# Last output layer of two chained MLPs: six of its seven token tiles as seven block products instead of eight, the sums of h and of weights made by GpSimd

## The chip, the cores and the metric

The kernel runs on one core of a Trainium2 chip. Its time is the device time of one execution in microseconds (us); lower is better. TensorE (PE in the profile) does the matmuls into PSUM banks, VectorE (DVE) and ScalarE (ACT) the elementwise work, GpSimd (POOL) is a third elementwise engine that takes its operands from SBUF, and SyncE (SP) issues the DMAs. Each engine works through its own queue in order and waits on semaphores of the others.

## The reference

Attention with mixed heads gives x of 1792 tokens by 768; two MLPs follow, and the output of the second is the result:

```
h = x @ w_in;    g = elu(h);        x = g @ w_out       # first MLP,  768 -> 2048 -> 768
h = x @ w_in2;   g = relu(h)**2;  out = g @ w_out2      # second MLP, 768 -> 2048 -> 768
```

All arrays are float32 at the kernel's door. This case is about the last product, `g @ w_out2`, for the second half of the tokens (896 of them).

## The kernel before, in words

Attention comes first, then both MLPs for the first 896 tokens, then both for the second 896. Each float32 operand of a matmul is split into a high part (`hi`, a cast to fp32r) and a low part (`lo` = the value minus `hi`, also fp32r), and a product is three matmuls: hi by hi, lo by hi, hi by lo (`three`, L661 to L666). The cast is ACT's (L518 for weights, L669 for h), the subtraction is DVE's (L525 for weights, L670 for h), and both inputs of that subtraction lie in SBUF.

The last stage is `outer_last(1)` (L935). h is kept raw in 16 tiles `hr`, one for each block of 128 of the 2048 rows of the inner dimension, 896 tokens wide. For each half `nh` of the 768 output columns and each of the 16 blocks `f`, one weight tile (128 by 384) and one h tile are split, and for each of the seven token tiles of 128 three matmuls with 384 columns are issued, the h part being the stationary operand: 2 x 16 x 7 x 3 = 672 matmuls. At the end of each half seven banks are copied out, by DVE and ACT in turn, and stored. Weights come from DRAM (`w2of`) through six buffers `wf`; a buffer can be loaded again when its `hi` and `lo` have been made. The parts lie in five buffers `wh`/`wl` and four `rh`/`rl`, which TensorE frees. `Weights.load_ahead` sets how far ahead loads are issued, `Weights.part` makes the two parts of the next weight tile, `split_ahead` those of the next h tile.

The stage ahead of it, `seven(1, ...)` (L732), makes h with seven block products (Strassen's scheme in Winograd's form); its last pieces end on DVE in lines L753 to L801 (sums of a PSUM bank and a saved tile) and L693 (squares, both inputs in SBUF).

Of the kernel before, what the change touches and what calls it, by code (L numbers as in the profile page):

```python
# [8 lines left out]
F32 = mybir.dt.float32  # L9
# [15 lines left out]
FU = DM // 2  # L25
# [356 lines left out]
class Weights:  # L382
# [5 lines left out]
    def __init__(self, nc, dram, w1i, w1o, w2i, w2o):  # L388
# [14 lines left out]
        for k in (k1i, k2i):  # L403
            self.units += [(name, k, q, STATIONARY) for q in range(FC // 2) for name in self.SEVEN]
            if k is k1i:
                self.units += [("f32", k1o[:, f, t * FU : (t + 1) * FU], None, STATIONARY) for t in range(2) for f in range(FC)]
        self.units += kept
        self.raw, self.single, self.parts, self.keep, self.quad, self.aside, self.extra = {}, {}, {}, [], {}, [], []
# [8 lines left out]
    def load(self, room=None):  # L417
        i = self.loaded
        self.loaded += 1
        kind, src, kept, _ = self.units[i]  # L420
        if kind == "f64":
            self.raw[i] = self.load_raw(src, room)
        elif kind == "f32":
            self.single[i] = self.plain()
            self.nc.sync.dma_start(out=self.single[i], in_=src)
        elif kind == "a11":
            of = self.quad[kept, id(src)] = {}
            for j, name in ((2, "a21"), (3, "a22"), (0, "a11"), (1, "a12")):
                of[name] = self.plain("aq", 4) if j < 2 else self.plain()
                self.nc.sync.dma_start(out=of[name], in_=src[4 * kept + j])  # L430
# [78 lines left out]
    def part_hi(self):  # L509
        i = self.done  # L510
        kind, start = self.units[i][0], self.units[i][3]
        if kind in self.SEVEN:
            self.single[i] = self.combine(*self.units[i][1:3], kind)
        f = self.single[i]
        n = f.shape[1]
# [18 lines left out]
    def load_ahead(self, i):  # L534
        self.flush()
        while self.loaded < len(self.units):
            if self.loaded > i + (self.LOAD if self.units[self.loaded][0] not in self.SEVEN else len(self.SEVEN)):
                break
            self.load()
# [23 lines left out]
def col(i):  # L563
    return slice(i * 128, (i + 1) * 128)


class Mlps:
# [164 lines left out]
    def seven(self, m, x, carry=()):  # L732
# [23 lines left out]
        for q in range(FC // 2):  # L756
            a, b, c, d, e = (self.bank()[:, :S] for _ in range(5))
            plan = (("b11", a), ("t1", b), ("b21", a), ("b22", b), ("t2", c), ("t3", d), ("t4", e))
            for i, (name, p) in enumerate(plan):
# [50 lines left out]
                del carry[:3]  # L810
                if q == FC // 2 - 1 and i in (2, 4):
                    self.split_ahead(i // 4)
        for step in range(7 * FC // 2, 7 * FC // 2 + 3):
# [121 lines left out]
    def outer_last(self, half):  # L935
# [28 lines left out]
        return x if half == 0 else None  # L964

    def run(self):
        with ExitStack() as ctx:
# [22 lines left out]
        self.hr = {}  # L990
        self.start_split(STATIONARY)
        self.seven(1, x, carry)
        self.outer_last(1)

# [48 lines left out]
```

## Time and profile before

| | us |
|---|---|
| median of 3 runs (lowest to highest) | 1278.42 (1274.05 to 1279.73) |
| the profiled execution, its own time | 1277.57 |
| its span, first to last instruction | 1275.7 |
| PE busy in the span | 1233.7 |
| DVE, ACT, POOL busy | 943.1, 679.3, 52.4 |
| mean granted clock of TensorE | 0.996 of full speed |

The time of the profiled execution lies 1.87 us above its span, which is what is around the instructions. Matmul durations in the records overlap each other (each is pipelined into the next), so for TensorE the distance from one start to the next is read, not the duration.

### The profile page before, as it was taken

Reading aid. Unit: us, or ns where it says so; the run is one execution under the profiler, and the core shown is the slowest. Engines: PE = TensorE matmul, PEld = TensorE weight load, DVE = VectorE, ACT = ScalarE, POOL = GpSimd, SP = SyncE. Lnnn points to the kernel's source line nnn. Section 1 sums busy time; section 2 is a strip of 40 time slices with the busy share of each in tenths; the row PEclk is TensorE's granted clock in tenths of the full one; section 3 lists DMA queues with packets and bytes.
Section 4 is the critical chain, followed back from the end, with each engine's and each line's share of the span. In section 5 each row is a group of like instructions: output and inputs, shape, how many; then the busy total and the mean of one; then the engine's idle time right before and its main releaser. Section 6 shows DMA issues by size and latency. Waiting matters only on the chain.

```text
span 1275.7 us, 35064 instructions
## 1 busy us (share of the span) xinstructions
PE 1233.7 (97%) x14295; PEld 1101.7 (86%) x14296; DVE 943.1 (74%) x1974; ACT 679.3 (53%) x1476; POOL 52.4 (4%) x118
## 2 busy tenths in 40 slices
PE   9999989999789999999999999999999999999998
PEld 4677777777579999988899999999999998999998
DVE  4577667777759998778999996868874559887452
ACT  4666666666537774333444554546663445454342
POOL 1011010110410000000000000000000000000000
PEclk9999999999999999999999999999999999999999
DMA  6666646555635545666666555131221111212131
GB/s 186 201 204 195 208 161 205 185 171 184 203 108 177 174 155 162 191 184 199 224 222 227 186 174 171 49 119 50 69 75 55 51 50 50 75 44 85 34 105 44
DMA packets 124121, 179.02 MB, mean 140 GB/s; under 512 B 25177, under 2 KB 103353, under 8 KB 123961
## 3 DMA queue, kind: packets, MB, share of 16 engines
q1 hardware_dynamic: 123720, 176.50, 43.0%
q8 instruction: 112, 1.84, 0.6%
q14 instruction: 49, 0.39, 0.1%
q10 hardware_dynamic: 240, 0.29, 0.1%
HBM read 101.86 MB, written 36.18 MB: 108 GB/s over the span
## 4 chain that ended last, share of the span: by engine, by line
PE 76%; DVE 11%; ACT 6%; DMA 3%; issue 3%; SPq 0%; ACTq 0%; DVEq 0%; POOL 0%; POOLq 0%
PE ps_qk L664 5%; PE ps_qk L666 5%; PE ps_qk L665 5%; PE ps_pv L665 5%; PE ps_pv L666 5%; PE ps_pv L664 5%; PE ps_post L664 5%; PE ps_post L666 5%; PE ps_post L665 5%; PE ps_mix L664 5%; PE ps_mix L666 5%; PE ps_mix L665 5%; PE ps_mix L182 4%; PE ps_post L218 4%; PE ps_pv L254 3%; PE ps_qk L156 3%
## 5 line engine op out<-in xcount | busy, mean ns | idle before, releaser
L518 ACT CAST wh<-wf 128x384 fp32r<-128x384 f32 (+1 forms) x272 | 133.3, 492 | 209.6 <-DVE wf L477 129.4
L525 DVE TENSOR_TENSOR wl<-wf,wh 128x384 fp32r<-128x384 f32 (+1 forms) x272 | 144.7, 534 | 76.4 <-ACT wh L518 74.7
L218 PEld LDWEIGHTS ps_post<-wg,ex 60*64 60x64 f32 x5040 | 139.5, 135 | 51.2 <-issue 30.2
L192 ACT ACTIVATE ex<-ps_mix,nmax 128x448 f32<-128x448 f32 x180 | 112.6, 630 | 117.5 <-DVE nmax L190 117.4
L670 DVE TENSOR_TENSOR rl<-hr,rh 128x896 fp32r<-128x896 f32 x96 | 104.5, 1089 | 54.4 <-ACT rh L669 54.4
L218 PE MATMUL ps_post<-wg,ex 60*64 60x60 f32 x5040 | 135.0, 220 | 6.5 <-issue 4.9
L236 DVE COPY at<-ps_post 128x420 f32<-128x420 f32 x178 | 97.6, 591 | 53.8 <-PE ps_post L218 51.1
L182 PE MATMUL ps_mix<-graw,pre 64*64 64x448 f32 (+1 forms) x720 | 113.6, 557 | 13.8 <-ACT ex L192 6.3
L190 DVE TENSOR_REDUCE nmax<-ps_mix 128x1 f32<-128x448 f32 x180 | 104.5, 616 | 24.3 <-PE ps_mix L182 23.9
L669 ACT CAST rh<-hr 128x896 fp32r<-128x896 f32 x96 | 90.1, 939 | 50.3 <-PE ps_post L666 25.1
L254 PE MATMUL ps_pv<-at,v 64*64 64x110 f32 (+3 forms) x2976 | 100.0, 249 | 5.3 <-issue 2.9
L254 PEld LDWEIGHTS ps_pv<-at,v 64*64 64x64 f32 x2976 | 88.4, 134 | 14.9 <-issue 6.5
L156 PE MATMUL ps_qk<-kt,qt 64*64 64x448 f32 (+1 forms) x680 | 92.6, 543 | 1.5 <-ACT sc L161 1.2
L447 ACT ACTIVATE wf<-wd 128x384 f32<-128x384 f32 (+1 forms) x134 | 68.1, 512 | 42.8 <-DMA wd<-w1o 24.0
L161 ACT COPY sc<-ps_qk 120x448 f32<-120x448 f32 x167 | 80.7, 539 | 11.1 <-PE ps_qk L156 11.1
L477 DVE SCALAR_TENSOR_TENSOR wf<-wd,wf 128x384 int32<-128x384 int32 (+1 forms) x134 | 67.7, 509 | 3.9
L475 DVE SCALAR_TENSOR_TENSOR wf<-wd,wf 128x384 int32<-128x384 int32 (+1 forms) x134 | 67.7, 509 | 3.8
L182 PEld LDWEIGHTS ps_mix<-graw,pre 64*64 64x64 f32 (+1 forms) x720 | 34.7, 134 | 32.7 <-ACT ex L192 16.6
L684 ACT ACTIVATE tmp<-tmp 128x448 f32<-128x448 f32 x48 | 27.9, 581 | 57.2 <-DVE tmp L794 43.9
L664 PE MATMUL ps_qk<-xh,wh 128*128 128x448 f32 x150 | 55.3, 369 | 0.3 <-DVE tmp L691 0.3
L666 PE MATMUL ps_qk<-xh,wl 128*128 128x448 f32 x150 | 55.0, 367 | 0.0
L665 PE MATMUL ps_qk<-xl,wh 128*128 128x448 f32 x150 | 55.0, 367 | 0.0
(247 smaller groups left out, 3152.1 us busy)
## 6 DMA issues: line engine op xcount, KB each, us to landing
graw<-sc SPq DMA_DIRECT2D x180, 210.0 KB
wd<-w1i SPq DMA_DIRECT2D x32, 384.0 KB
wd<-w1o SPq DMA_DIRECT2D x48, 256.0 KB
wd<-w2i SPq DMA_DIRECT2D x32, 384.0 KB
wf<-w2of SPq DMA_DIRECT2D x48, 192.0 KB
wd<-w2o SPq DMA_DIRECT2D x22, 384.0 KB
w1if<-wf SPq DMA_DIRECT2D x32, 192.0 KB
w1of<-wf SPq DMA_DIRECT2D x48, 128.0 KB
```

The source lines that it names most:

```text
L156: nc.tensor.matmul(out[a][x:y], qt[n][o, p, x:y], k[o, p, :], start=True, stop=True)
L182: nc.tensor.matmul(out[r][64 * g : 64 * g + 64], pre64[o], e[g][o], start=True, stop=True)
L190: nc.vector.tensor_reduce(nmax, p, AX.X, ALU.max, negate=True)
L192: nc.scalar.activation(e, p, AF.Exp, bias=nmax, scale=1.0, accum_out=tot[s][:, r : r + 1])
L218: nc.tensor.matmul(out[g][y, 6 if c == 3 else 2 * c + r], e[rows][o, key : key + 64], w[o, rows], start=True, stop=True)
L254: nc.tensor.matmul(p, vt[b, i // 3][y, jc, g % 6 * D : (g % 6 + 1) * D], m, start=(jc == 0), stop=(jc == JC - 1), skip_group_check=True)
L518: self.nc.scalar.copy(hi, f)
L525: self.nc.vector.tensor_tensor(lo, self.single.pop(i), hi.bitcast(F32), ALU.subtract)
L664: mm(p, wh, xh, start=first, stop=False)
L665: mm(p, wh, xl, start=False, stop=False)
L666: mm(p, wl, xh, start=False, stop=last)
L670: self.nc.vector.tensor_tensor(lo, raw, hi.bitcast(F32), ALU.subtract)
```

## The change

The 896 tokens are seven tiles of 128. Tiles 0 to 2 and tiles 4 to 6 become the two row blocks of a 2 by 2 block product (A11, A12 and A21, A22 of h, cut along the inner dimension after block 8; B11, B12, B21, B22 of the weights, cut likewise and at column 384); tile 3 is multiplied as before. The seven products are, in this order: n = 0, A11 B11; n = 1, S1 T1; n = 2, A12 B21; n = 3, S4 B22; n = 4, S2 T2; n = 5, S3 T3; n = 6, A22 T4. Each has 8 steps, one for each inner block. The sums S (of h) and T (of weights) are made by GpSimd in float32 from the raw tiles, and ACT and DVE split them as they split raw tiles. For that the raw weights are kept until GpSimd has read them, and B12 and B21 are loaded a second time into a `spare` of four tiles. Tile 3 takes part in n = 0 (with B11 and B12), 2 and 3. The blocks of the output are put together from banks and saved tiles at the end of each product, by ACT, DVE and, in six places, GpSimd.

```
-        self.units += kept
+        first, second = kept[:FC], kept[FC:]
+        self.made, self.keep_raw, self.k2o = {}, {}, k2o
+        half = FC // 2
+        self.units += [u for f in range(half) for u in (first[f], second[f])]
+        self.units += [("made", ("t1", f), None, MOVING) for f in range(half)]
+        self.units += first[half:] + second[half:]
+        self.units += [("made", (name, f), None, MOVING) for name in ("t2", "t3", "t4") for f in range(half)]
+        self.last = len(self.units) - 8 * half
...
+            if i >= self.last:
+                self.keep_raw[i] = self.single[i]
...
+            if self.loaded >= self.last and self.loaded > i + self.LOAD - 1:
+                break
...
-                if q == FC // 2 - 1 and i in (2, 4):
-                    self.split_ahead(i // 4)
+                if q == FC // 2 - 1 and i in (2, 4, 6):
+                    if m == 0:
+                        if i < 6:
+                            self.split_ahead(i // 4)
+                    else:
+                        self.part_last(0, i // 2 - 1)
...
+    def part_last(self, n, f):
+        a = (STATIONARY - H_AT) % LINE // 4
+        t = self.sums[f] if n in (1, 4) else self.hr[f + (FC // 2 if n in (2, 3, 6) else 0)]
+        t = t[:, 512:] if n == 6 else t[:, : 512 if n in (0, 2, 3) else 384]
+        parts = [self.hq.tile([128, 2 * S + LINE // 4], F32R, name=f"r{x}", bufs=4)[:, a : a + t.shape[1]] for x in "hl"]
+        self.split(*parts, t)
+        self.halves[n, f] = parts
+    def seven_last(self):
...
+        for k, (n, f) in enumerate(steps):
...
+            if n == 0:
+                weights = [w.take(), w.take()]
+            else:
+                weights = [w.take()]
+            taken.append((f, hi, lo, weights))
+            tail = n == 6 and half - 3 <= f < half - 1
+            if not tail:
+                for i in range(3):
+                    for g, hi, lo, weights in taken:
+                        self.three(p[i], hi[:, col(i)], lo[:, col(i)], *weights[0], n not in (2, 3) and g == 0,
+                                   n in (2, 3, 4, 5, 6) and g == half - 1, True)
+                    if n == 6 and f == half - 1:
+                        o = room()
+                        tt(o, u[i], p[i], ALU.subtract)
+                        put(o, 4 + i, 0)
+                if n in (0, 2, 3):
+                    for j, y in enumerate(weights):
+                        q = j if n == 0 else n - 2
+                        self.three(rest[q], hi[:, col(3)], lo[:, col(3)], *y, n == 0 and f == 0, n > 0 and f == half - 1, True)
+                taken.clear()
+            if n == 0:
+                sub(ta[f], w.keep_raw[at + 1], w.keep_raw[at], ALU.subtract)
+                sub(self.sums[f], self.hr[f][:, 512:], self.hr[f + half][:, 512:], ALU.add)
+            elif n == 1:
+                sub(self.sums[f], self.sums[f], self.hr[f][:, :FU], ALU.subtract)
+            elif n == 2:
+                sub(self.hr[f + half][:, :FU], self.hr[f + half][:, :FU], self.sums[f], ALU.subtract)
+            elif n == 3:
+                sub(ta[f], w.keep_raw[at], ta[f], ALU.subtract)
+                sub(tb[f], w.keep_raw[at], aux["b12", f], ALU.subtract)
+            elif n == 4:
+                sub(self.hr[f][:, :FU], self.hr[f][:, :FU], self.hr[f][:, 512:], ALU.subtract)
+            if (n, f) >= (5, 1) and (k - 41) < half:
+                sub(ta[k - 41], ta[k - 41], aux["b21", k - 41], ALU.subtract)
+            if 21 <= k < 21 + half:
+                load("b12", k - 21, FC + k - 21)
+            if 38 <= k < 38 + half:
+                load("b21", k - 38, half + k - 38)
+            w.load_ahead(w.used)
+            while w.done < min(len(w.units), w.used + 4):
+                w.part()
+            if k + 3 < len(steps):
+                self.part_last(*steps[k + 3])
+            if f < half - 1:
+                continue
+            for i in range(3):
+                if n == 0:
+                    copy(one_a[i], p[i])
+                elif n == 1:
+                    copy(one_b[i], p[i])
+                elif n == 2:
+                    out(p[i], i, 0, copies[i % 2])
+                elif n == 3:
+                    copy(both[i], p[i])
+                elif n == 4:
+                    tt(u[i], p[i], one_a[i], ALU.add)
+                    o = room()
+                    sub(o, both[i], u[i], ALU.add)
+                    put(o, i, 1)
+                elif n == 5:
+                    tt(u[i], p[i], u[i], ALU.add)
+                    o = room()
+                    sub(o, u[i], one_b[i], ALU.add)
+                    put(o, 4 + i, 1)
+            if n in (2, 3):
+                out(rest[n - 2], 3, n - 2, copies[n - 2])
...
-        self.start_split(STATIONARY)
+        self.halves, self.k2o = {}, w.k2o
         self.seven(1, x, carry)
-        self.outer_last(1)
+        self.seven_last()
```

In the changed kernel the same helpers stand 11 to 13 lines lower (L529 and L536 split weights, L682 and L683 split h, L677 to L679 are the three matmuls). `sub` is GpSimd's tensor_tensor, `tt` is DVE's.

Where instructions stand now. GpSimd's queue, at the start of the last stage, before: after the weighing of attention's last step (`wg`) there is nothing but the end of the program.

```order
L659 TENSOR_TENSOR xl_6961<-tmp_7343,xh_6960 128x448
L202 TENSOR_TENSOR wg_7617<-post_87,rec_7615 128x120
L1039 UNCONDITIONAL_BRANCH
```

The same place in the changed kernel, the first four of 70 new instructions of this kind, and the first four of n = 3 (`xh` and `xl` are the rooms of the sums, `wf` raw weights, `hr` raw h):

```order
L202 TENSOR_TENSOR wg_7617<-post_87,rec_7615 128x120
L1059 TENSOR_TENSOR xh_15966<-wf_15877,wf_15854 128x384
L1060 TENSOR_TENSOR xl_15967<-hr_14955,hr_15491 128x384
L1059 TENSOR_TENSOR xh_15966<-wf_15915,wf_15895 128x384
L1060 TENSOR_TENSOR xl_15967<-hr_15008,hr_15544 128x384
...
L1066 TENSOR_TENSOR xh_15966<-wf_16461,xh_15966 128x384
L1067 TENSOR_TENSOR xl_15967<-wf_16461,xh_15966 128x384
L1066 TENSOR_TENSOR xh_15966<-wf_16484,xh_15966 128x384
L1067 TENSOR_TENSOR xl_15967<-wf_16484,xh_15966 128x384
```

DVE's queue, from the last square of the stage ahead into the first steps of the last stage, before:

```order
L693 TENSOR_TENSOR hr_15956<-tmp_15959 128x448
L525 TENSOR_TENSOR wl_15974<-wf_15879,wh_15973 128x384
L525 TENSOR_TENSOR wl_15978<-wf_15897,wh_15977 128x384
L670 TENSOR_TENSOR rl_15982<-hr_15089,rh_15981 128x896
L525 TENSOR_TENSOR wl_16009<-wf_15917,wh_16008 128x384
L670 TENSOR_TENSOR rl_16013<-hr_15142,rh_16012 128x896
```

And in the changed kernel; a step of n = 0 now takes two weight tiles and one narrower h tile, and four weight parts stand ahead of the first of these h tiles:

```order
L706 TENSOR_TENSOR hr_15954<-tmp_15961 128x448
L536 TENSOR_TENSOR wl_15999<-wf_15895,wh_15998 128x384
L536 TENSOR_TENSOR wl_16003<-wf_15915,wh_16002 128x384
L536 TENSOR_TENSOR wl_16007<-wf_15936,wh_16006 128x384
L536 TENSOR_TENSOR wl_16011<-wf_15992,wh_16010 128x384
L683 TENSOR_TENSOR rl_16015<-hr_15142,rh_16014 128x512
L536 TENSOR_TENSOR wl_16040<-wf_15994,wh_16039 128x384
L536 TENSOR_TENSOR wl_16044<-wf_15996,wh_16043 128x384
L683 TENSOR_TENSOR rl_16048<-hr_15223,rh_16047 128x512
```

SyncE's queue in the changed kernel around the end of n = 2 (`wf` are first loads of weights, `xh` second loads into `spare`, `out` the four stores of that end): a second load of B12 and the first loads of B22's last two tiles now stand behind the four stores.

```order
L434 DMA wf_16579<-w2of_68 128x384
L1017 DMA out<-tmp_16589 128x384
L1017 DMA out<-tmp_16592 128x384
L1017 DMA out<-tmp_16595 128x384
L1017 DMA out<-tmp_16598 128x384
L1013 DMA xh_15966<-w2of_68 128x384
L434 DMA wf_16616<-w2of_68 128x384
```

## Rows read from the trace of the kernel before

**Rows 1.** The page, part 1: busy us, share of the span, instructions.

```profile
PE 1233.7 (97%) x14295; PEld 1101.7 (86%) x14296; DVE 943.1 (74%) x1974; ACT 679.3 (53%) x1476; POOL 52.4 (4%) x118
```

**Rows 2.** Windows of the last stage: us, busy of each engine, clock, DMA.

```profile
1155.20:1213.40 58.20, 58.20 (x337) 58.19 (x337) 30.70 (x42) 24.18 (x38) 0.00 (x0) 1.00 0.21 64
1213.40:1271.90 58.50, 58.47 (x338) 58.15 (x336) 24.50 (x31) 20.03 (x31) 0.00 (x0) 1.00 0.18 59
```

**Rows 3.** Timeline of PE, first and last matmuls of the stage: start, us, engine.

```profile
1155.03 0.36 PE L666 MATMUL ps_qk<-eh,wl 128*128 128x448 f32 x1
1155.23 0.34 PE L664 MATMUL ps_mix<-wh,rh 128*128 128x384 f32 x1
1155.40 0.34 PE L665 MATMUL ps_mix<-wl,rh 128*128 128x384 f32 x1
...
1271.53 0.34 PE L666 MATMUL ps_post<-wh,rl 128*128 128x384 f32 x1
```

**Rows 4.** Groups of the last stage by form: count, busy us, mean ns, idle before.

```profile
L670 DVE TENSOR_TENSOR rl<-hr,rh 128x896 fp32r<-128x896 f32 x30 | 32.7, 1091 | 9.0 <-ACT rh L669 9.0
L669 ACT CAST rh<-hr 128x896 fp32r<-128x896 f32 x30 | 28.1, 937 | 2.1 <-PE ps_post L665 2.1
L525 DVE TENSOR_TENSOR wl<-wf,wh 128x384 fp32r<-128x384 f32 x31 | 17.2, 556 | 38.3 <-ACT wh L518 38.3
L518 ACT CAST wh<-wf 128x384 fp32r<-128x384 f32 x30 | 15.3, 512 | 53.0 <-PE ps_pv L666 27.4 <-PE ps_post L666 24.0 <-issue 1.7
```

**Rows 5.** Timeline, 349 to 352 us and 329 us: DVE beside POOL.

```profile
349.32 1.15 POOL L659 TENSOR_TENSOR xl<-tmp,xh 128x448 fp32r<-128x448 f32 x1 [6.60 <-ACT xh L658]
350.15 0.72 DVE L525 TENSOR_TENSOR wl<-wf,wh 128x384 fp32r<-128x384 f32 x1 [0.84 <-ACT wh L518]
350.42 1.46 POOL L659 TENSOR_TENSOR xl<-tmp,xh 128x448 fp32r<-128x448 f32 x1
350.80 1.49 DVE L525 TENSOR_TENSOR wl<-wf,wh 128x384 fp32r<-128x384 f32 x1
...
329.56 2.22 POOL L659 TENSOR_TENSOR xl<-tmp,xh 128x448 fp32r<-128x448 f32 x2 [2.07 <-DMA tmp<-xd]
329.85 0.87 DVE L197 TENSOR_SCALAR tot<-tot 128x2 f32<-128x2 f32 x1
```

**Rows 6.** Timeline of DVE into the last stage, before.

```profile
1151.36 1.08 DVE L670 TENSOR_TENSOR rl<-hr,rh 128x896 fp32r<-128x896 f32 x1
1152.37 0.61 DVE L793 TENSOR_TENSOR tmp<-ps_post,tmp 128x448 f32<-128x448 f32 x1
...
1155.21 0.55 DVE L525 TENSOR_TENSOR wl<-wf,wh 128x384 fp32r<-128x384 f32 x1
1155.68 0.61 DVE L753 TENSOR_TENSOR tmp<-tmp,ps_qk 128x448 f32<-128x448 f32 x1
1156.21 1.69 DVE L693 TENSOR_TENSOR hr<-tmp 128x448 f32<-128x448 f32 x3
...
1158.29 0.55 DVE L525 TENSOR_TENSOR wl<-wf,wh 128x384 fp32r<-128x384 f32 x1
1158.76 1.08 DVE L670 TENSOR_TENSOR rl<-hr,rh 128x896 fp32r<-128x896 f32 x1
1159.76 0.55 DVE L525 TENSOR_TENSOR wl<-wf,wh 128x384 fp32r<-128x384 f32 x1
```

**Rows 7.** Weight loads: SP's issue, then GB/s from 1140 to 1160 us in half-us slices.

```profile
1148.46 0.32 SPq L425 DMA_DIRECT2D wf<-w2of  x1
...
GB/s 0 0 0 0 0 0 0 0 0 0 0 0 0 0 0 0 0 0 22 169 203 0 25 249 363 151 0 0 0 0 126 264 3 87 243 80 0 0 58 280
```

**Rows 8.** Single lines, ns min/median/max: L659; L525 in the last stage; L197.

```profile
L659 POOL TENSOR_TENSOR xl<-tmp,xh x12: 1122/1136/1455, 329.6 to 356.2; 128x448 fp32r<-128x448 f32 x12
L525 DVE TENSOR_TENSOR wl<-wf,wh x34: 549/557/559, 1149.9 to 1254.2; 128x384 fp32r<-128x384 f32 x34
L197 DVE TENSOR_SCALAR tot<-tot x90: 156/160/874, 23.1 to 354.6; 128x2 f32<-128x2 f32 x90
```

**Rows 9.** POOL's groups by form over the whole span.

```profile
L202 POOL TENSOR_TENSOR wg<-post,rec 128x120 f32<-128x120 f32 x90 | 34.8, 387 | 291.2 <-DVE rec L199 221.2 <-PE ps_mix L182 61.1 <-PE ps_qk L156 8.9
L659 POOL TENSOR_TENSOR xl<-tmp,xh 128x448 fp32r<-128x448 f32 x12 | 13.7, 1162 | 13.6 <-ACT xh L658 11.5 <-DMA tmp<-xd 2.1
```

**Rows 10.** Timeline of the end, before.

```profile
1271.91 0.56 DVE L961 COPY tmp<-ps_post 128x384 f32<-128x384 f32 x1 [0.48 <-PE ps_post L666]
```

More of the change, by code (lines that the diff above doesn't have):

```diff
@@ L513, in part_hi @@
             self.single[i] = self.combine(*self.units[i][1:3], kind)
+        if kind == "made":
+            self.single[i] = self.made[self.units[i][1]]
         f = self.single[i]
@@ L964, in outer_last, with rooms, load, put @@
         return x if half == 0 else None
+    def part_last(self, n, f):
[6 more added lines that the diff above has]
+    def seven_last(self):
+        nc, w = self.nc, self.weights
+        copy, tt, sub = nc.scalar.copy, nc.vector.tensor_tensor, nc.gpsimd.tensor_tensor
+        k2o, half = self.k2o, FC // 2
+        def rooms(pool, tag, n):
+            room = pool.tile([128, n], F32, name=tag, tag=tag)
+            return [room[:, i * FU : (i + 1) * FU] for i in range(n // FU)]
+        high, low = (rooms(self.xp, f"x{x}", KC * 2 * S + LINE // 4) for x in "hl")
+        ta, spare, tb, self.sums = high[:8], high[8:12], low[:8], low[8:14] + high[12:14]
+        kept = [rooms(self.ep, f"e{x}", 9 * S) for x in "hl"]
+        one_a, one_b, both, u = kept[0][:3], kept[0][3:6], kept[0][6:9], kept[1][:3]
+        for name, of in (("t1", ta), ("t2", ta), ("t3", tb), ("t4", ta)):
+            for f in range(half):
+                w.made[name, f] = of[f]
+        aux = {}
+        def load(name, f, i):
+            aux[name, f] = spare[f % 4]
+            nc.sync.dma_start(out=spare[f % 4], in_=k2o[i])
+        def put(o, i, nh):
+            r = 2 * S + i * 128
+            nc.sync.dma_start(out=self.out[r : r + 128, nh * FU : (nh + 1) * FU], in_=o)
+        def room():
+            return self.tmp()[:, :FU]
+        def out(p, i, nh, engine):
+            o = room()
+            engine(o, p)
+            put(o, i, nh)
+        copies = nc.vector.tensor_copy, copy
+        steps = [(n, f) for n in range(7) for f in range(half)]
+        banks = [[self.bank()[:, :FU] for _ in range(3)]]
+        rest = [self.bank()[:, :FU] for _ in range(2)]
+        taken = []
+        for k, (n, f) in enumerate(steps):
+            at = w.used
+            hi, lo = self.halves.pop((n, f))
+            if f == 0 and n in (1, 4, 5, 6):
+                banks.append([self.bank()[:, :FU] for _ in range(3)])
+            p = banks[(0, 1, 0, 1, 2, 3, 4)[n]]
+            if n == 0:
[59 more added lines that the diff above has]
+                    tt(u[i], p[i], u[i], ALU.add)
+                    o = room()
+                    sub(o, u[i], one_b[i], ALU.add)
+                    put(o, 4 + i, 1)
+            if n in (2, 3):
+                out(rest[n - 2], 3, n - 2, copies[n - 2])
```

## The prediction

> **What bounds the kernel now.** First the page's busy times [rows 1]: PE works in 97% of the span, so what counts is what reaches PE. Then the windows of the last stage [rows 2]: PE is busy in all but 0.03 us of 116.7 at a granted clock of 1.00, DVE in 55.2, ACT in 44.2, POOL in none. The stage is bound by matmuls alone. Its timeline [rows 3] gives the price of one: from the first start, 1155.23, to the last of 672, 1271.53, is 116.30 us over 671 distances, 0.1733 us each. The groups [rows 4] say what feeds it: one h part (DVE 1.09 us) and one weight part (0.56 us) for every 3.64 us of matmuls, with waits on DVE and ACT that are theirs, not PE's. From the page alone, fewer matmuls would be time won. But the change hands 70 sums to POOL, and the last view to read is how POOL and DVE run side by side [rows 5].
>
> **What it removes.** Product 0 has 15 matmuls a step (three tiles, and tile 3 with two weight tiles), products 2 and 3 have 12, products 1, 4, 5 and 6 have 9: 8 x (15 + 24 + 36) = 600 instead of 672. At 0.1733 us [rows 3], 72 matmuls are **12.5 us**, and a step lasts 2.60, 2.08 or 1.56 us on PE: 104.0 us in all.
>
> **What it adds on ACT and DVE.** 64 weight tiles are split instead of 32, and 56 h tiles of 512 (24 of them) or 384 columns instead of 32 of 896. DVE takes 0.47 us from the start of a 384-column part to that of the next instruction (1158.29 to 1158.76) and 1.00 for 896 (1158.76 to 1159.76) [rows 6], so 0.60 for 512: some 118 parts are about 60 us, plus 9 for banks, of 104. ACT stays below that [rows 4]. Alone, both hide under PE, but for the start: the third weight tile is wanted after 15 matmuls, at 1157.8, while DVE still has the squares of the stage ahead to do (1156.21 and 1.69 us long [rows 6]). Two h parts ahead of them become 0.4 us shorter, one of 0.6 is added: the part would be there at about 1158.2. That costs 0.4 us.
>
> **What it adds on DMA.** 16 second loads of 192 KB, and the same 14 stores. DMA engines are busy for 0.21 and 0.18 of the stage [rows 2], so the amount is free. A load takes some 2.0 us: issued at 1148.46, its bytes move in the slices up to 1150.5 [rows 7]. The place in the queue is not free, see product 3.
>
> **What it adds on POOL, and what that does to DVE.** The span has no POOL sum of 384 columns. 448 columns take 1136 ns (median [rows 8]), 120 take 387 [rows 9]: 2.28 ns a column, so 384 take 0.99 us. 70 of them are 69 us of 104, which alone would hide. The trace shows that they are not alone. While two POOL sums ran, two weight parts of DVE, 0.56 us at any time in the last stage [rows 8], took 0.72 and 1.49, and the second POOL sum 1.46 [rows 5]. Taking each undisturbed length from its end gives when it really began: DVE 350.32, POOL 350.74, DVE 351.74. So they took turns: DVE's part kept POOL away for 0.42 us, POOL's sum of 448 columns kept DVE away for 1.00. Scaled to 384 columns POOL holds for 0.86 us; a DVE part of 512 holds for 0.56. A tiny DVE operation shows the same: 0.87 us beside a POOL sum [rows 5], 0.16 usually [rows 8]. Every weight part and h part of the last stage reads two SBUF tiles, as the held ones did; so do the squares. DVE's operations that read a bank did not show it.
>
> The Trainium skill, "SBUF — State Buffer", section "Who interferes with whom", states this as a rule against such a change: a DVE instruction with two SBUF inputs and a GpSimd instruction that reads SBUF use one shared read interface under an exclusive lock, kept for the whole instruction. That they take turns, the trace agrees [rows 5]. By "the whole instruction" a pair would cost the recorded 0.56 + 0.99 = 1.55 us and the sum would be the long-hold rival below; by the rows it is 1.28. The measurement decides.
>
> **The sum in turns.** In us a step, DVE's holds and POOL's against PE's: product 0, 1.40 + 1.72 = 3.12 against 2.60; product 1, 0.84 + 0.86 = 1.70 against 1.56; product 2, 0.98 + 0.86 = 1.84 against 2.08; product 3, 0.98 + 1.72 = 2.70 against 2.08; products 4 and 5, 1.70 against 1.56; product 6, 0.84 against 1.56. What decides is how many sums stand ready, because each ready one delays one DVE part: then a step of two parts costs 2.56 to 2.70 us, and the lead of two to three steps that the buffers allow is used up. By product:
>
> Product 0. POOL may start at about 1150.0, when PE has read the last of the tiles whose room the sums take. Six sums find their data there, 5.2 us of holds; four DVE operations on banks (0.6 each) hide about two of them. The third weight part comes at about 1161.1 instead of 1158.2, and PE's second step 3.3 us late. In the other seven steps 0.52 us each is missing, 3.6; 1.4 of it the lead covers. Together **+5.5**.
>
> Products 1 and 2. S2 overwrites S1, and S4 overwrites A12, which must be split before: POOL has one sum a step to do and DVE's lead rather pays 1 us and gets it back. **0**.
>
> Product 3. The 16 sums T2 and T3 and the 8 sums S3 wait for nothing that DVE does; some start in the second half of product 2. Eight steps at 2.70 instead of 2.08 are 5.0 late. In SP's queue the fourth second load of B12 and the last two first loads stand behind the four stores of product 2, whose copies stand behind delayed parts on DVE: POOL and then DVE stop until they land, some 2 us with neither at work. Product 2's lead gives 2.6 back. **+4.4**.
>
> Product 4. About nine sums are left, so five of its steps cost 2.56 instead of 1.56: 5.0, less 0.3 of lead, **+4.7**.
>
> Product 5. Three sums for stores and seven T4 are ready, again five steps at 2.56: 5.0, less 1.5 of lead, **+3.5**.
>
> Product 6. One sum is left; its part is wanted only at the last step. **0**. The end is as before: one DVE operation on a bank after the last matmul (1271.91 to 1272.47 [rows 10]) and a store.
>
> Added, 18.1 us; removed, 12.5. Against the profiled execution's own 1277.57 that is +5.6: **1283 us**, 0.36% above the median of the runs, 1278.42, which itself is 0.85 above that execution.
>
> **The bounds.** Below: if port and engines never stop, the holds decide. All eight-step sums are 108.8, six sums for stores 5.2, squares and one other of the stage ahead 2.4; without product 6 (6.7), in which PE is the slower one, and the h part already made (0.6), 109.1 us from 1150.0 is 1259.1, and product 6 adds 12.5: PE ends at 1271.6, as it does now (1271.7). That is 1277.5 us. Above: 0.27 us more for each of 70 pairs by recorded lengths is 19 us: 1302. The kind of work is that of [rows 5] (the same DVE instruction, POOL one size wider), so I stay near the holds that they show.
>
> **The rivals.**
> No turns: the meeting of [rows 5] was something else and the sums hide. For it: POOL has 35 us to spare, DVE 35. Against it: two independent DVE forms and POOL itself show it. Then 12.5 less 0.4: 1265.5 us, faster. Point of decision: DVE's weight parts stay at 0.56 us while POOL works.
> Tight turns: the 18.1 shrinks since POOL's early sums go into DVE's idle time and the lead never breaks. 1277.5 us, no change. Point of decision: the stops in products 3 and 5 don't appear.
> Long holds: a pair costs its recorded 1.55 us. For it: POOL's own records are rough, and a chain of alternate waits may lose something at each hand-over. Against it: the two turns of [rows 5]. 1302 us, slower. Point of decision: stage sum of DVE's and POOL's busy times equals its length.
>
> **How the numbers follow.** The turns as summed: 0.55, with a range of its own of 1277 to 1291 (half the lead's cover either way, and 0.1 us on each of 70 pairs). Tight turns 0.13, no turns 0.16, long holds 0.11, a wait that I don't see 0.05. A measurement of this kernel can tell about 0.5%, 6.4 us, from no change: below 1272.0 is faster, above 1284.8 slower. Faster is no turns, 0.16. Of the forecast's 0.55 some 0.36 lies below 1284.8; with tight turns that is the same, 0.49. Slower is 0.19 of the forecast, long holds and the unseen wait: 0.35. The range takes in no turns at its low end and reaches to 1293, where about 0.15 is left above it.
>
> **What the profile of the changed kernel would show.** The matmul count of the stage, 600, at 0.173 us where they run on. DVE's weight parts in the stage at a mean near 1 us instead of 0.56, with many at about 1.4 in products 0, 3, 4 and 5, and near 0.56 in product 6. PE's idle time in the stage near 18 us, ended by DVE's parts: a gap of some 3 us after the first step, none to speak of in products 1, 2 and 6. POOL sums at 0.99 us or, waiting, up to 1.4. A DVE mean near 0.56 there would refute the turns; PE gaps ended by POOL itself or by SP's loads would mean another wait than mine; a clock below 1.00 in these gaps would add what I have not counted.

## The result, and the profile after

| | kernel before | changed kernel |
|---|---|---|
| median (lowest to highest) of 15 executions of each | 1277.16 us (1270.61 to 1285.45) | 1282.98 us (1279.22 to 1292.57) |
| ratio of the two, with its 95% interval | | 1.0054 (1.0027 to 1.0080) |
| the profiled execution, its own time | 1277.57 us | 1292.57 us |
| first matmul of the last stage | 1155.23 us | 1164.44 us |
| length of the last stage on PE (first to last start, and one matmul more) | 116.47 us | 122.59 us |

The change makes the kernel 0.5% slower, by 5.8 us between the medians; 1283 us with +5.6 was forecast. The profiled execution of the changed kernel is the slowest of its 15. Of the 15.0 us by which it is longer than that of before, 9.2 lie ahead of the last stage, where they were not followed, and executions of the kernel before differ by as much among themselves. So the stage is compared, not the span: 122.59 - 116.47 = **6.1 us longer**, though it has 72 matmuls fewer.

The page of the changed kernel, its busy times (us, share of the span, instructions), answers to [rows 1]. The windows of the last stage below it answer to [rows 2], with the same columns.

```profile
PE 1240.2 (96%) x14224; PEld 1092.8 (85%) x14224; DVE 1001.6 (78%) x2034; ACT 696.0 (54%) x1537; POOL 141.0 (11%) x188
```

```profile
1164.40:1287.10 122.70, 110.77 (x602) 105.80 (x600) 113.88 (x133) 60.60 (x129) 83.56 (x67) 0.97 0.28 87
```

Before, PE was busy in all of this stage and DVE in half of it. Now PE stands still for 11.9 us of 122.7, its mean clock is 0.97, and DVE is busy in 113.9 us. A page that shows DVE at 93% with the other engines waiting for it seems to say that DVE has too much work. It does not, and the next two views tell why. The groups of DVE and POOL in the last stage (with columns as in [rows 4]):

```profile
L683 DVE TENSOR_TENSOR rl<-hr,rh 128x512 fp32r<-128x512 f32 x22 | 30.5, 1386 | 0.0
L536 DVE TENSOR_TENSOR wl<-wf,wh 128x384 fp32r<-128x384 f32 x31 | 25.7, 845 | 3.5 <-ACT wh L529 3.4
L536 DVE TENSOR_TENSOR wl<-xh,wh 128x384 fp32r<-128x384 f32 x24 | 20.2, 841 | 2.1 <-ACT wh L529 2.1
...
L1066 POOL TENSOR_TENSOR xh<-wf,xh 128x384 f32<-128x384 f32 x8 | 11.1, 1385 | 0.0
L1069 POOL TENSOR_TENSOR hr<-hr 128x384 f32<-128x384 f32 x8 | 10.3, 1319 | 0.0
```

The weight part of 384 columns, 0.56 us before [rows 4], has a mean of 0.84, and an h part of 512 takes 1.39. The timeline of DVE in product 4 (1241.4 to 1258.4 us on PE) shows that this mean is made of two lengths:

```profile
1247.16 1.36 DVE L536 TENSOR_TENSOR wl<-xh,wh 128x384 fp32r<-128x384 f32 x1
1248.45 1.36 DVE L683 TENSOR_TENSOR rl<-xl,rh 128x384 fp32r<-128x384 f32 x1
1249.73 1.35 DVE L536 TENSOR_TENSOR wl<-xh,wh 128x384 fp32r<-128x384 f32 x1
1251.01 1.36 DVE L683 TENSOR_TENSOR rl<-xl,rh 128x384 fp32r<-128x384 f32 x1
1252.30 0.55 DVE L536 TENSOR_TENSOR wl<-xh,wh 128x384 fp32r<-128x384 f32 x1
1252.76 0.55 DVE L683 TENSOR_TENSOR rl<-xl,rh 128x384 fp32r<-128x384 f32 x1
```

POOL beside it, the same stretch: eight sums S3 without a break, 1.29 us each.

```profile
1240.37 1.32 POOL L1067 TENSOR_TENSOR xl<-wf,xh 128x384 f32<-128x384 f32 x1
1241.66 10.30 POOL L1069 TENSOR_TENSOR hr<-hr 128x384 f32<-128x384 f32 x8
1259.26 3.60 POOL L1095 TENSOR_TENSOR tmp<-eh,el 128x384 f32<-128x384 f32 x3 [7.30 <-ACT wh L529]
```

While POOL works, a DVE part starts every 1.28 us (1249.73 - 1248.45, and 1251.01 - 1249.73), and POOL keeps the same beat: one for you, one for me. The moment POOL's last sum ends, at 1251.96, DVE's parts are 0.55 us again and start every 0.47. PE, which wants two parts every 1.56 us in products 4 and 5, then gets them every 2.57. Its timeline in product 4 (start, length, and in brackets the idle time and what ended it):

```profile
1244.73 0.44 PE L679 MATMUL ps_mix<-wh,rl 128*128 128x384 f32 x1 [0.73 <-DVE rl L683]
...
1247.29 0.44 PE L679 MATMUL ps_mix<-wh,rl 128*128 128x384 f32 x1 [0.73 <-DVE rl L683]
...
1249.86 0.44 PE L679 MATMUL ps_mix<-wh,rl 128*128 128x384 f32 x1 [0.73 <-DVE rl L683]
```

The two stops at the start of the stage are of another kind. Lines of PE there, and after them windows of 2 us (busy PE, PEld, DVE, ACT, POOL; then the granted clock):

```profile
1166.87 0.34 PE L679 MATMUL ps_mix<-wh,rl 128*128 128x384 f32 x1
1168.79 0.44 PE L677 MATMUL ps_mix<-wh,rh 128*128 128x384 f32 x1 [1.58 <-ACT wh L529]
1170.94 0.69 PE L678 MATMUL ps_mix<-wl,rh 128*128 128x384 f32 x1 [1.71 <-DVE wl L536]
...
1171.74 0.52 PE L677 MATMUL ps_post<-wh,rh 128*128 128x384 f32 x1
1172.06 0.52 PE L678 MATMUL ps_post<-wl,rh 128*128 128x384 f32 x1
...
1176.52 0.34 PE L677 MATMUL ps_post<-wh,rh 128*128 128x384 f32 x1
```

```profile
1166.00:1168.00 2.00, 1.21 (x7) 0.89 (x6) 2.00 (x3) 0.24 (x1) 2.00 (x2) 1.00 0.34 102
1168.00:1170.00 2.00, 0.44 (x1) 0.19 (x1) 2.00 (x4) 2.00 (x6) 0.79 (x2) 0.91 0.00 1
1170.00:1172.00 2.00, 1.06 (x3) 1.06 (x4) 2.00 (x2) 0.91 (x2) 1.74 (x2) 0.50 0.04 8
1172.00:1174.00 2.00, 2.00 (x8) 2.00 (x8) 2.00 (x5) 0.00 (x0) 0.00 (x0) 0.50 0.65 191
1174.00:1176.00 2.00, 2.00 (x8) 2.00 (x7) 0.76 (x3) 1.14 (x3) 1.38 (x2) 0.50 0.79 260
1176.00:1178.00 2.00, 2.00 (x12) 2.00 (x11) 2.00 (x3) 0.33 (x1) 2.00 (x2) 0.88 0.42 128
```

PE waits for the two parts of the second step's first weight tile, the third of the stage, and its clock falls to 0.50, the 1.2 GHz level. The matmuls that follow start every 0.32 us instead of 0.173, although PE shows as fully busy: a busy share does not tell a slow clock, the distance of starts does. The 17 distances from 1170.94 to 1176.52 take 5.58 us, 2.6 more than at 0.1733. Distances also tell more than the brackets, because a matmul's record is longer than its share of the time: the 0.73 us above cost 2.57 - 1.56 = 1.01.

The first of the two stops ends with a cast of ACT, whose casts keep their 0.51 us beside POOL. The rows of ACT and DVE ahead of it tell why:

```profile
1165.70 1.50 DVE L683 TENSOR_TENSOR rl<-hr,rh 128x512 fp32r<-128x512 f32 x1
1167.12 0.60 DVE L766 TENSOR_TENSOR tmp<-tmp,ps_qk 128x448 f32<-128x448 f32 x1
1167.76 0.58 ACT L697 ACTIVATE tmp<-tmp 128x448 f32<-128x448 f32 x1 [2.15 <-DVE tmp L766]
```

ACT's cast stands behind L697, L697 waits for DVE's L766, and L766 stands behind an h part that took 1.50 us beside POOL where it takes 0.68 alone. So this stop too goes back to parts that POOL held up. L766 itself, which reads a PSUM bank, kept its 0.6 us beside a POOL sum.

From the first matmul of one product to that of the next, less its matmuls at 0.1733 us, is how late PE became in it. For the kernels with block products, in us of their profiled executions (e1 to e10 are told below; the sums can differ from the parts by a rounding):

| product | 0 | 1 | 2 | 3 | 4 | 5 | 6 | sum |
|---|---|---|---|---|---|---|---|---|
| forecast | 5.5 | 0 | 0 | 4.4 | 4.7 | 3.5 | 0 | 18.1 |
| changed kernel | 6.36 | 0.0 | 0.0 | 4.07 | 4.53 | 2.78 | 0.86 | 18.6 |
| e1, sums on DVE | 2.45 | 0 | 0 | 0 | 0 | 0 | 1.43 | 3.9 |
| e3, only products 0 to 2 on POOL | 6.03 | 0 | 0.07 | 0 | 0 | 0.70 | 1.95 | 8.8 |
| e4, product 0's on DVE | 2.46 | 1.91 | 0.33 | 5.07 | 4.51 | 1.93 | 1.68 | 17.9 |
| e6, stores after loads | 5.97 | 0 | 0.05 | 3.83 | 3.71 | 1.94 | 1.66 | 17.2 |
| e5, on DVE, reordered | 2.21 | 0.55 | 0 | 0 | 0 | 0.05 | 0.19 | 3.0 |
| e10, e5 with S4 on POOL | 2.29 | 0.52 | 0.01 | 0 | 0 | 1.16 | 0.17 | 4.2 |

### The profile page after: what moved, and what is told of

It reads as the page before. It is cut to its first block, busy times and chain, and to the rows that moved or that the text cites. A ratio compares the mean times of both kernels' runs of the same rounds, so it can differ in the third digit from the quotient of the medians.

```text
span 1290.7 us, 35231 instructions
## 1 busy us (share of the span) xinstructions
PE 1240.2 (96%) x14224; PEld 1092.8 (85%) x14224; DVE 1001.6 (78%) x2034; ACT 696.0 (54%) x1537; POOL 141.0 (11%) x188
## 3 DMA queue, kind: packets, MB, share of 16 engines
q8 instruction: 112, 1.84, 0.6%
## 4 chain that ended last, share of the span: by engine, by line
PE 73%; DVE 14%; ACT 6%; issue 4%; DMA 3%; SPq 0%; ACTq 0%; POOL 0%; DVEq 0%; POOLq 0%
PE ps_qk L677 5%; PE ps_qk L679 5%; PE ps_qk L678 5%; PE ps_mix L182 5%; PE ps_pv L678 5%; PE ps_pv L679 5%; PE ps_pv L677 5%; PE ps_mix L679 5%; PE ps_mix L678 5%; PE ps_post L677 4%; PE ps_mix L677 4%; PE ps_post L678 4%; PE ps_post L679 4%; PE ps_post L218 4%; PE ps_pv L254 4%
## 5 line engine op out<-in xcount | busy, mean ns | idle before, releaser
L529 ACT CAST wh<-wf 128x384 fp32r<-128x384 f32 (+1 forms) x272 | 133.0, 491 | 183.2 <-DVE wf L486 128.8
L536 DVE TENSOR_TENSOR wl<-wf,wh 128x384 fp32r<-128x384 f32 (+1 forms) x272 | 153.6, 568 | 42.0 <-ACT wh L529 40.3
L683 DVE TENSOR_TENSOR rl<-hr,rh 128x896 fp32r<-128x896 f32 (+2 forms) x104 | 115.9, 1116 | 46.3 <-ACT rh L682 46.3
L190 DVE TENSOR_REDUCE nmax<-ps_mix 128x1 f32<-128x448 f32 x180 | 104.5, 616 | 24.0 <-PE ps_mix L182 23.5
L682 ACT CAST rh<-hr 128x896 fp32r<-128x896 f32 (+2 forms) x104 | 82.8, 798 | 49.6 <-PE ps_post L679 25.1
L1059 POOL TENSOR_TENSOR xh<-wf 128x384 f32<-128x384 f32 x8 | 11.2, 1401 | 806.8 <-DVE wl L536 802.1
L156 PE MATMUL ps_qk<-kt,qt 64*56 64x448 f32 (+1 forms) x680 | 92.1, 543 | 1.6 <-ACT sc L161 1.2
L202 POOL TENSOR_TENSOR wg<-post,rec 128x120 f32<-128x120 f32 x90 | 34.7, 387 | 291.8 <-DVE rec L199 222.1
L697 ACT ACTIVATE tmp<-tmp 128x448 f32<-128x448 f32 x48 | 27.8, 579 | 59.4 <-DVE tmp L807 43.8
L677 PE MATMUL ps_qk<-xh,wh 128*128 128x448 f32 x150 | 55.6, 371 | 0.0
```

The source lines that it names most:

```text
L190: nc.vector.tensor_reduce(nmax, p, AX.X, ALU.max, negate=True)
L529: self.nc.scalar.copy(hi, f)
L536: self.nc.vector.tensor_tensor(lo, self.single.pop(i), hi.bitcast(F32), ALU.subtract)
L677: mm(p, wh, xh, start=first, stop=False)
L683: self.nc.vector.tensor_tensor(lo, raw, hi.bitcast(F32), ALU.subtract)
```

## The experiments

The theory is the forecast's: DVE's parts and POOL's sums take turns at SBUF, 1.28 us a pair, and what a step then needs is more than PE's time for it. The rivals are that the stage is late for another reason (DVE overloaded by more and smaller parts, the longer chain of loads), and that single stops (the start, SP's queue) make up the loss.

### e1: the same sums on DVE

```
-        copy, tt, sub = nc.scalar.copy, nc.vector.tensor_tensor, nc.gpsimd.tensor_tensor
+        copy, tt, sub = nc.scalar.copy, nc.vector.tensor_tensor, nc.vector.tensor_tensor
```

> All 76 sums (70 in the stage's steps and ends, as counted with the six for stores) go to DVE instead of POOL, at the same places of the program. Turns theory: no part waits any more, a sum costs DVE 0.47 us, and each step still fits under PE (product 0: 2.48 of 2.60 us, 1: 1.41 of 1.56, 2: 1.54 of 2.08, 3: 2.01 of 2.08, 4 and 5: 1.41 of 1.56). The last stage lasts 105 to 108 us instead of 122.6, with 1 to 3 us lost at its start; DVE's weight parts are back at 0.55 us; the time is about 15 us under the changed kernel, some 9 under the kernel before. Rival, that the block scheme itself (order of loads, two weight tiles a step, stores in SP's queue) costs the time: the stage stays above 116 us. Rival, that DVE becomes the bound since it now carries some 100 us of work in 104: the stage lasts 110 to 116 us, with PE waiting for DVE's parts in every product.

(The sums number 70, with the six for stores.) Measured: 1272.94 us against 1280.44, ratio 0.9941 (0.9914 to 0.9968), so 7.5 us under the kernel before where some 9 were expected; late 3.9 us instead of 18.6. The windows of its last stage:

```profile
1157.40:1265.30 107.90, 104.83 (x601) 103.73 (x599) 99.97 (x202) 60.58 (x129) 0.00 (x0) 1.00 0.32 100
```

DVE does 69 instructions more than in the changed kernel (202 against 133) and is busy for 14 us less. Not one matmul of products 1 to 5 waits. The work was never too much for DVE: its busy time in the changed kernel was in part waiting, recorded as work. This refutes that smaller parts or loads are the cause of the 14.7 us that went. The 3.9 that stay, at the start and in product 6, are not POOL's; e5 looks at them.

### e2, e8, e9: POOL's sums without the block product

In these three the kernel before keeps its 672 matmuls, and POOL makes sums of h beside it whose results nobody reads. The three differ in when POOL may begin. There are 72 sums in e2 and 67 in e8 and e9, where the expectations count 70. e2, after the matmuls of a step (the lines that make room for the results are left out here):

```
...
+                if half == 1:
+                    for i in range(3 if f % 5 == 0 else 2):
+                        nc.gpsimd.tensor_tensor(self.beside[i], self.hr[f][:, :n2], self.hr[f][:, 512:], ALU.add)
```

> The kernel before, its computation whole, with 70 POOL sums of two raw h tiles (384 columns, result unused, nobody waits for it) put beside its last stage, two or three a step. Turns theory: DVE's weight parts rise from 0.56 us to about 0.9 to 1.4 and its h parts from 1.09 to about 1.5 in that stage, POOL's sums take 1.2 to 1.5 instead of 0.99; but a step of that stage has 3.64 us on PE and the turns in it only need 0.96 + 0.42 + 2 x 0.86 = 3.1, so PE loses nothing: stage 116 to 118 us, time as before within 0.3%. No-turns rival: DVE's parts stay at 0.56 and 1.09. Rival that POOL work slows TensorE or DMA itself: the stage is longer than 120 us.

Measured: 1285.56 us against 1280.44, ratio 1.0056 (1.0027 to 1.0084). No change was expected, and that missed: the stage takes 120.9 us, which meets the condition of the second rival (longer than 120). From 1165 to 1262 us the weight part has a mean of 1.29 us and the h part of 896 columns 1.89, where 0.56 and 1.09 stood [rows 4], as the turns say. But the loss, 4.4 us, is one stop at the start, 2.64 us at 1173.05, and the half clock after it; the stage's second half is 0.01 us late, though the sums run until 1263.9. Nothing ties these sums to their steps, since all of h lies ready: they ran one after another from 5 us ahead of the stage on, on top of the squares and the first parts. e8 places them two steps later in the program:

```
-                if half == 1:
+                if half == 1 and s > 1:
```

> The kernel before with POOL sums beside its last stage as in the earlier run of this kind, but from the third step on, after DVE has done the last work of the stage ahead. Turns theory: the gap of 2.6 us on PE and the half clock behind it go, the stage is 116.5 to 117 us, while DVE's weight parts stay near 1.29 us and its h parts near 1.9; the time as before within 0.3%. Rival, that POOL's sums cost PE time by another way than DVE's parts: the stage stays above 119 us.

Measured: 1284.88 us against 1279.54, ratio 1.0039 (1.0014 to 1.0064), with the same stop of 2.63 us and a stage of 121.2, above the 119 that the rival asked for. The edit had no effect of the kind that it was made for: POOL's queue holds nothing else, so a later place in the program is no later time. It tells nothing between the theories. e9 gives each sum the `hi` part of its own step as an operand, which ties it to the step:

```
-                        nc.gpsimd.tensor_tensor(self.beside[i], self.hr[f][:, :n2], self.hr[f][:, 512:], ALU.add)
+                        nc.gpsimd.tensor_tensor(self.beside[i], self.hr[f][:, :n2], hi[:, :n2].bitcast(F32), ALU.add)
```

> As the run before of this kind, the kernel before with unused POOL sums beside its last stage, but each sum reads the step's own high part of h, so that it can't start before ACT has made that part: the sums then come two or three a step, as DVE's parts do, and none meets the last work of the stage ahead. Turns theory: DVE's weight parts near 0.9 to 1.3 us, its h parts near 1.5 to 1.9, POOL's sums 1.2 to 1.5, and PE late by less than 1 us: stage 116.5 to 117.5, since a step needs 3.1 of 3.64 us. Rival, that POOL's sums cost PE time by another way: the stage stays above 119 us and PE's waits are spread over the steps.

Measured: 1278.42 us against 1279.13, ratio 0.9985 (0.9957 to 1.0013). The stage takes 116.5 us, as in the kernel before, and the rival falls. Windows and groups of 1170 to 1260 us:

```profile
1170.00:1260.00 90.00, 90.00 (x521) 90.00 (x521) 67.62 (x54) 34.30 (x52) 86.50 (x61) 1.00 0.19 58
```

```profile
L670 DVE TENSOR_TENSOR rl<-hr,rh 128x896 fp32r<-128x896 f32 x25 | 43.0, 1720 | 2.1 <-ACT rh L669 1.9
L525 DVE TENSOR_TENSOR wl<-wf,wh 128x384 fp32r<-128x384 f32 x25 | 24.2, 968 | 17.6 <-ACT wh L518 17.6
```

POOL is busy for 86.5 of 90 us, both parts of DVE are 0.4 to 0.6 us longer, and PE waits for nothing: the two parts need 2.69 us and a step of the kernel before gives them 3.64. Turns alone cost nothing; turns where a step has less time than they take cost the difference, once the lead is used up.

### e3 and e4: part of the sums on POOL

```
+            sub = (nc.gpsimd if n < 3 else nc.vector).tensor_tensor
```

> Sums of products 0 to 2 stay on POOL, those made in products 3 to 6 (T2, T3, S3, T4, six for stores) go to DVE. Turns theory: the late time on PE by product, 6.4, 0, 0, 4.1, 4.5, 2.8, 0.9 us in the changed kernel, becomes 6.4, 0, 0 and then less than 1 each; stage 111 to 113 us. Structure rival: products 3 to 5 stay late by 3 us or more each, since stores and second loads stand in the same order in SP's queue.

Measured: 1275.07 us against 1280.44, ratio 0.9964 (0.9933 to 0.9996). The stage takes 112.7 us, as expected. The 11.4 us of products 3 to 5 are gone but for 0.7; product 0 stays 6.0 late, with the same two stops (1.59 and 1.70 us) and a clock of 0.50 after them. e4 is the other half:

```
+            sub = (nc.vector if n < 1 else nc.gpsimd).tensor_tensor
```

> Only the 16 sums of product 0 go to DVE. Turns theory: product 0 is late by 1 to 3 us instead of 6.4 (DVE has 0.9 us more to do ahead of the third weight part), the gap after the first step shrinks below 2 us, TensorE keeps its clock at 1.00 there, products 3 to 5 stay late by 4, 4.5 and 3; stage 116 to 119 us. Rival, that the start is late because four weight parts now stand ahead: product 0 stays late by 5 us or more.

One execution, 1293.60 us with the stage beginning at 1166.25: product 0 is 2.5 late instead of 6.4, with stops of 0.36 and 1.56 us and no slow clock, and products 3 to 5 are 11.5 late as in the changed kernel. Product 1 loses 1.9 that it did not before, and product 6 0.8 more, so the sum hardly falls, and the stage of 121.9 us misses the expected 116 to 119. DVE's rows in product 1 of e4:

```profile
1195.90 1.36 DVE L683 TENSOR_TENSOR rl<-xl,rh 128x384 fp32r<-128x384 f32 x1
1197.18 0.55 DVE L536 TENSOR_TENSOR wl<-xh,wh 128x384 fp32r<-128x384 f32 x1
1197.65 1.36 DVE L683 TENSOR_TENSOR rl<-xl,rh 128x384 fp32r<-128x384 f32 x1
```

POOL's one sum a step holds up one of the two parts, and a step takes 1.75 us (1197.65 - 1195.90) against PE's 1.56. So product 1 does lose when no lead covers it; in the changed kernel it lost nothing at the same work. That DVE has no lead left here because it made product 0's sums itself is likely and not shown. e3 shows that the loss of products 3 to 5 goes with the sums made there; e4 shows the same of 3.9 us in product 0, though 3.2 of them come back later.

### e6: the first stores of the stage behind the loads

The stores of column half 0 are kept back until step 4 of product 3, so that no second load of B12 and no first load of weights stands behind them in SP's queue:

```
...
-            put(o, i, nh)
+            if nh == 0:
+                later.append((o, i, nh))
+            else:
+                put(o, i, nh)
...
+            if (n, f) == (3, 4):
+                for x in later:
+                    put(*x)
```

> The changed kernel, sums on POOL, with the four stores of product 2 (and those after it to the first column half that go through the same helper) put behind the second loads of B12 and the last first loads of weights in SP's queue. The prediction's step: the stop of POOL at the fourth second load (2.8 us there) goes, and product 3 is late by some 2 us less than 4.1. Since POOL's sums then only come earlier and each still delays a part, a rival: product 3 stays late by 4 us or more, the stop having cost nothing of its own. Both: products 4 and 5 are late by 3 to 5 us each, the stage within 2 us of 122.6.

One execution, 1285.73 us. In the changed kernel POOL waited 2.76 us for a second load of B12; some 2 were forecast:

```profile
1226.23 1.32 POOL L1066 TENSOR_TENSOR xh<-wf,xh 128x384 f32<-128x384 f32 x1
1230.32 1.01 POOL L1067 TENSOR_TENSOR xl<-wf,xh 128x384 f32<-128x384 f32 x1 [2.76 <-DMA xh<-w2of]
```

In e6 this wait is gone, and product 3 is 3.83 us late instead of 4.07. PE's timeline in e6 shows why:

```profile
1222.88 0.44 PE L679 MATMUL ps_post<-wh,rl 128*128 128x384 f32 x1 [1.07 <-DVE rl L683]
1225.58 0.45 PE L679 MATMUL ps_post<-wh,rl 128*128 128x384 f32 x1 [0.35 <-DVE rl L683]
1228.29 0.44 PE L679 MATMUL ps_post<-wh,rl 128*128 128x384 f32 x1 [0.31 <-DVE rl L683]
1231.00 0.44 PE L679 MATMUL ps_post<-wh,rl 128*128 128x384 f32 x1 [0.36 <-DVE rl L683]
```

From here on every step of product 3 takes some 2.7 us (1225.58 - 1222.88), the pace of the turns (forecast 2.70), instead of one long stop. The expectation, some 2 us less in product 3, missed; the rival, no gain there, is nearly what came. From product 3 to the end, e6 is 11.1 us late against 12.2. So the stop is worth some 1.1 of the 2 us that the forecast gave it, and little of it in product 3; product 0, which the edit does not touch, differs by 0.4 between these two executions.

### e5: all sums on DVE, and none ahead of what PE waits for

e1 was late at the start and in product 6. In e5 the third weight tile's parts are made before the first sums, S1's sum comes after the h part, and the sums of product 5's stores wait until step 5 of product 6 (shown in part; `sub` is DVE's as in e1, and the three sums leave their old place):

```
...
             if n == 0:
+                while w.done < w.used + 2:
+                    w.part()
                 sub(ta[f], w.keep_raw[at + 1], w.keep_raw[at], ALU.subtract)
-                sub(self.sums[f], self.hr[f][:, 512:], self.hr[f + half][:, 512:], ALU.add)
...
+            if n == 0:
+                sub(self.sums[f], self.hr[f][:, 512:], self.hr[f + half][:, 512:], ALU.add)
+            if (n, f) == (6, 5):
+                for i in range(3):
+                    o = room()
+                    sub(o, u5[i], one_b[i], ALU.add)
+                    put(o, 4 + i, 1)
...
```

> All 70 sums on DVE, and two places reordered: in product 0 a step's next two weight parts come ahead of the sum T1, and S1 after the h part; the three sums for the stores of product 5 come after the last h part instead of ahead of the last four. Turns theory: with no turns, what is left late (2.5 us in product 0, 1.4 in product 6 when all sums are on DVE in the old order) is DVE's order alone; product 0 late by 0.3 to 1.2, product 6 by less than 0.5, the stage 104.5 to 106 us instead of 107.9; the time some 10 to 12 us under the kernel before, ratio 0.990 to 0.993. Rival, that the start is late because of the weights' loads: product 0 stays late by 2 us or more.

Measured: **1267.64 us** against 1279.54, ratio 0.9908 (0.9873 to 0.9943), faster than both kernels. The stage takes 107.0 us where 104.5 to 106 was expected. Product 6 lost its delay (0.2 instead of 1.4); product 0 kept 2.2, above the 2 that the rival, late loads, asked for. In its first two steps it loses 1.5. What holds it there (DVE and PE, start and length):

```profile
1157.04 0.69 DVE L683 TENSOR_TENSOR rl<-hr,rh 128x512 fp32r<-128x512 f32 x1 [0.68 <-ACT rh L682]
1157.65 0.62 DVE L766 TENSOR_TENSOR tmp<-tmp,ps_qk 128x448 f32<-128x448 f32 x1
1158.18 1.69 DVE L706 TENSOR_TENSOR hr<-tmp 128x448 f32<-128x448 f32 x3
1159.79 1.02 DVE L536 TENSOR_TENSOR wl<-wf,wh 128x384 fp32r<-128x384 f32 x2
```

```profile
1159.34 0.44 PE L677 MATMUL ps_mix<-wh,rh 128*128 128x384 f32 x1 [0.36 <-ACT wh L529]
1160.40 0.44 PE L678 MATMUL ps_mix<-wl,rh 128*128 128x384 f32 x1 [0.62 <-DVE wl L536]
```

The weight part that PE waits for stands on DVE behind the last pieces of the stage ahead (L766, and the squares of L706), not behind a sum, and these pieces stand behind an h part that waited 0.68 us for ACT. The other 0.7 us of product 0, in its last three steps, come behind a weight load that ACT waits for, so the rival is right in part:

```profile
1175.54 0.51 ACT L529 CAST wh<-wf 128x384 fp32r<-128x384 f32 x1 [1.87 <-DMA wf<-w2of]
```

DVE makes the part behind this cast at 1176.08, and PE waits for it at 1176.69. Product 1, which lost nothing in e1, loses 0.55 here.

### e10: e5, but S4 on POOL

```
+            sub = (nc.gpsimd if n == 2 else nc.vector).tensor_tensor
```

> The reordered version with all sums on DVE, but the 8 sums S4 of product 2 on POOL, where turns need 1.84 of 2.08 us a step. Turns theory: DVE's parts beside them take 0.7 to 1.0 us, POOL's sums 1.2, and product 2 is late by 0.0 as before; the stage stays at 106 to 108 us. Rival, that any POOL sum beside the parts costs PE time: products 2 or 3 are late by 1 us or more.

One execution, 1277.53 us with the stage beginning at 1163.83; its length is 108.1 us (e5: 107.0; 106 to 108 was expected). Product 2 is 0.01 late with its eight sums on POOL, as the forecast's 1.84 us of turns against 2.08 of PE say, and product 3 is not late either, so the rival falls. Product 5 lost 1.2 that e5 did not; from one execution this is left open. There is nothing to win here.

## Why the prediction was right

**Fewer matmuls, 12.5 us.** Right: 600, and where they run on they start every 0.173 us. e5 keeps 9.5 us of the 12.5 in its stage (107.0 against the stage of before, 116.5).

**The turns, 1.28 us a pair.** Right in kind and size. DVE and POOL start a part every 1.28 to 1.29 us when both are ready, two parts of 384 take 2.57 us (forecast 2.56), and a step of product 3 some 2.7 in e6 (2.70). The holds worked out from one meeting of two sums with two parts [rows 5] carried the whole forecast. By the rule of the Trainium skill, "SBUF — State Buffer", section "Who interferes with whom", read as a lock over the whole recorded instruction, a pair would by estimate have been 1.55 us and the kernel at 1302; that one engine waits while the other reads, the trace agrees, and the lock is shorter than the record. A step is late by what the turns need beyond PE's time, less what the lead covers: e9 shows the same contention hidden under 3.64 us, e1 the same work without it. The three rivals fall by this: no turns by the 1.36 us parts, tight turns by the stops in products 3 to 5, long holds by the beat of 1.28.

**DVE's mean.** Nearer 0.85 us than the forecast 1: the parts in saturated stretches are 1.36, as said, but fewer parts met a POOL sum. In product 6, where 0.56 was forecast, the mean is 0.70. PE's recorded idle time is 11.9 us where 18 was forecast; the rest of the 18.6 is in the slow clock and in matmul records that are longer than their share.

**Product 0, +5.5.** Measured 6.4. After the first step PE was 3.7 us late (1170.94 instead of 1167.22), forecast 3.3. The rest, 2.2 by DVE's pace, was put down wrongly. The 17 matmuls from 1170.94 on, at the 1.2 GHz level, cost 2.6 us; that cost the forecast named and did not count. 3.7 and 2.6 are the whole 6.4 but for rounding: from the fourth step on PE was not late at all, and in e3 and e6, whose product 0 is the same program, it lost some 0.6 there. So 2.2 for the pace was too much, and that the slow clock cost about as much is luck. e4, whose two stops are 0.36 and 1.56 us, keeps a clock of 1.00 and a product 0 of 2.5. The 0.4 for the start without sums was too little: e5 loses 1.5 in its first two steps.

**Product 3, +4.4.** Measured 4.1, with the stop of SP's queue where it was forecast, but e6 shows that this term was no addition: without the stop, eight steps at 2.71 instead of 2.08 give 5.0, of which the lead covered 1.2 (5.0 - 3.83) and not 2.6. Two errors, 2 us for the stop and a lead 1.4 too large, nearly cancelled, by luck.

**Products 4 and 5, +8.2.** Measured 7.3, at the pace forecast; product 5 has fewer slow steps than the five assumed, since POOL was idle from 1251.96 to 1259.26 and DVE undisturbed.

**Product 6, 0.** Measured 0.9: sums of T4 and for stores reached into it until 1280.6. e5, with all sums on DVE and the store sums moved, has 0.2.

**The whole.** 18.6 us late against 18.1, stage 6.1 us longer against 5.6, medians 5.8 apart. Single terms were off by up to 0.9 us, and not all for the reasons given. The mechanism and the 1.28 us are shown; that 1283 and the median agree to a tenth of a us is luck, since errors of single terms cancel and executions of the changed kernel differ by 13 us.

## What to carry to other kernels

Before elementwise work is moved from a busy VectorE to an idle GpSimd, look in the trace for a moment at which both work on two SBUF inputs, and add both engines' holds for each step; if the sum exceeds what TensorE gives a step, the move loses as soon as the lead is used up (product 1, 1.70 against 1.56, lost nothing in the changed kernel and 1.9 us in e4). Sums that stand ready early can cost a stop even where the steps have room (e2). Here 70 sums cost 33 us of DVE's own time (0.47 us each) and left it busy for 99 of e5's 107 us, while on the idle engine the same sums made the stage some 15 us longer than e1's and e5's. When an engine shows as 93% busy, compare the length of its instruction with the same instruction where it ran alone: a wait for memory is recorded as work. And try the dull placement too: e5, on one engine and in the order in which things are wanted, beat both kernels.

## What the runs showed that was not expected

- **The clock after short stops.** Two stops of 1.58 and 1.71 us with one matmul between them (1.59 and 1.70 in e3) came with a granted clock of 0.50, as did a single stop of 2.64 us (e2) and one of 2.63 (e8); 0.36 and 1.56 (e1, e4) or 0.36 and 0.62 us (e5) were not.
- **GpSimd's first sum.** After some 800 us without work its first sum took 2.39 us in the changed kernel, 3.10 in e2, 4.96 in e9 and 6.03 in e10, against 1.01 for an undisturbed one. In the changed kernel it began 5 us ahead of the stage. In these four it ended 0.87 to 0.88 us after DVE's unbroken row of operations with two SBUF inputs, the distance that the turns have too (a DVE part ends at 1251.08 in the rows above, POOL's sum beside it at 1251.96); until then DVE's operations kept the lengths that they have alone. In e10 the row ends at 1204.70 and the sum at 1205.58 (1199.56 + 6.03, rounded), and from then on they take turns:

```profile
1199.56 6.03 POOL L1066 TENSOR_TENSOR hr<-hr,xl 128x384 f32<-128x384 f32 x1 [839.04 <-DVE rl L683]
1204.03 0.67 DVE L683 TENSOR_TENSOR rl<-hr,rh 128x512 fp32r<-128x512 f32 x1
1204.83 1.17 DVE L536 TENSOR_TENSOR wl<-wf,wh 128x384 fp32r<-128x384 f32 x1
```

  So the recorded length of such a sum is nearly all waiting, and one engine ran at full speed while the other stood: that speaks for a lock, and against a bandwidth that both share. But strict turns hold only from the second sum on. In e4 the first sum took 1.17 us, let in after one DVE operation; why there and not in the others is open.
- **Program order is no time.** An instruction put two steps later on an otherwise idle engine ran as early as before (e8); only an operand of its step ties it there (e9).
